# Second layer of three experts with weights stationary and tokens moving, and a second ring of raw expert weights

## The chip, the cores and the metric

The kernel runs on one core of one Trainium2 chip. The metric is device microseconds (us) of one execution, the median of several runs.

## The reference, cut to what matters

Attention with a threshold (4 x 8 heads, 576 places, 64 wide), then a dense layer of 2048 hidden units on the 2304 tokens of 512 numbers, then a layer of eight experts of which each token goes through one. The change touches the experts:

```python
e_idx = np.argmax(x @ w_gate, axis=1)
for e in range(8):
    mask = e_idx == e
    h = np.maximum(x[mask] @ w1[e], 0.0)      # 512 -> 1024
    ye = h @ w2[e]                            # 1024 -> 512
    out[mask] = gate_w[mask, None] * eom[mask, e, None] * ye
```

In the attention, scores below the row's maximum less tau are left out of the softmax:

```python
thresh = np.max(scores, axis=-1, keepdims=True) - tau
scores = np.where(scores >= thresh, scores, -1000000000.0)
```

## The kernel before, in words

**Stages.** Attention and a first part of the dense layer run mixed (to about 510 us), then the rest of the dense layer with the gates (to about 765 us), then the experts one after another. Nothing is emitted where it stands: the program collects operations with `sc.add(engine, duration, due, function, reads, writes)`, and a planner (`Sched`) sorts them. It simulates the engines with the durations given, so that each figure in an `sc.add` and in helpers such as `pool_tt`, `dve`, `act` and `mm` bears on the order of instructions on every engine. `dma` adds the issuing instruction (500 ns on SP, 1038 ns on POOL) and an entry "DQ" for the transfer, whose latency the planner knows. Buffers come in rings (`buf(pool, name, n, shape)`), and the n-th buffer behind one waits for all its users; the turn within a ring follows the order in which the program creates buffers. On the chip each engine works through its own instructions in the planner's order. Products are taken in three parts, of high and low halves: high x high, high x low, low x high.

**Experts.** Experts 1 to 7 are ordered by load and have room for 384, 384, 352, 320, 288, 288 and 256 tokens (`CAPS`, the first of its eight entries is expert 0's), thus expert 4 has tiles of 128, 128 and 64, experts 5 and 6 of 128, 128 and 32. `expert(e)` (L1459) does this:
- Tokens: a gather of rows per tile (L1473, POOL), turned by PE (L1480, 4 transposes into "pt", a ring of two PSUM banks), rounded into xh (ScalarE) and the rest into xl (VectorE).
- First layer (L1537): for each of 8 blocks of hidden units, 3 products x 4 pieces of 128 inputs; a 128x128 piece of w1 is stationary and the tokens (the cap) move, into "ph", a ring of two PSUM banks. ScalarE takes relu to hh (L1542), VectorE the rest to hl (L1544); so hidden units lie across the partitions.
- Second layer (L1565): for each block f and token tile j, three matmuls in which the tile's hh or hl is stationary (128 hidden units x tokens) and the 512 columns of w2 move, into bank "py" of tile j:

```python
for n, (x_, wx) in enumerate(((h_, w_h), (h_, w_l), (l_, w_h))):
    nc.tensor.matmul(py[j].t[0:size[j]], x_(), wx(), ...)
```

- Then ScalarE scales each tile by its tokens' gates to "o" (L1573), and POOL scatters the rows to the output (L1577).

**Weights.** `raw_of` (L1302) gathers 512 KB of raw weights, enough for two of the sixteen pieces of an expert, with an indirect transfer issued on POOL (L1316), into "wraw", a ring of two buffers. `weights` splits each piece into a high part (ScalarE L420 and VectorE L424 in turn) and a low part (VectorE L440), into a set of 23 buffers.

**Thresholds.** In `attention`, each tile of scores gets its maximum on VectorE (L959, with the em tile), the exponential on ScalarE (L962, e) and the threshold tb = maximum + tau on GpSimd (L970, one column); then VectorE masks and sums (L972) from em, tb and e. Which engine takes tb is the table entry `"thr": "P"`, whose letters are taken in turn (A: ScalarE, D: VectorE, P: GpSimd).

Of the kernel before, what the change touches and what calls it, by code (L numbers as in the profile page):

```python
# [16 lines left out]
AF = mybir.ActivationFunctionType  # L17
# [4 lines left out]
P = 128  # L22
# [28 lines left out]
NHH = 12  # L51
NRAW = 2
ENGINES = {
# [3 lines left out]
    "r_3": "PD", "p_x": "Z" * 50 + "X" * 10 + "Z" + "XX" + "Z" + "X" * 62 + "Z" + "X", "bot": "A", "sum": "D",  # L57
# [216 lines left out]
def pool_tt(n):  # L274
    return int(2.11 * n + (145 if n > 400 else 12))

# [41 lines left out]
def tile_main(ctx, tc, qa, qb, q0, kT, vv, tau, w_in, w_out, gates, w1, w2, out, dbg=None):  # L318
# [108 lines left out]
    def rest(cls, n, due, dst, src, hi, r, w, psum=False):  # L427
        eng = pick(cls) if cls in ENGINES else cls
        if eng == "POOL" and n > HALVE:
            def part(k):  # L430
                a, b, h_ = dst(), src(), hi().bitcast(F32)
                m = a.shape[1]
                cut = slice(0, (m + 1) // 2) if k == 0 else slice((m + 1) // 2, m)
                nc.gpsimd.tensor_tensor(out=a[:, cut], in0=b[:, cut], in1=h_[:, cut], op=ALU.subtract)

            for k in range(2):
                o = sc.add("POOL", pool_tt(n // 2) + 170, due, lambda k=k: part(k), r, w)
            return o
        e = nc.vector if eng == "DVE" else nc.gpsimd
        return sc.add(eng, dve(n, psum) + 5 if eng == "DVE" else pool_tt(n), due, lambda: e.tensor_tensor(  # L440
            out=dst(), in0=src(), in1=hi().bitcast(F32), op=ALU.subtract), r, w, port=not psum)

    def dma(due, fn, r, w, nbytes, eng="SP", slack=0, after=()):
        o = sc.add(eng, 1038 if eng == "POOL" else 500, due, fn, r, w, lat=480, after=after)
        if due < 0 and not after:
            opening.append(o)
        sc.add("DQ", nbytes // 250, due, lambda: None, r, w, lat=810 + slack)
        return o
# [141 lines left out]
    def step(c, p, first, last, hp, xp, due, span, low, half, wide=False):  # L590
# [17 lines left out]
        for j in range(2):  # L608
            for n, (w_, x_) in enumerate(((0, xh), (0, xl), (1, xh))):
                sc.add("PE", 460, due + k * q, lambda j=j, n=n, w_=w_, x_=x_: hmm(j, n, w_, x_), [wi, x_], [ph])  # L610
                k += 1
# [31 lines left out]
        for t in range(2):  # L643
            for n, (g_, w_) in enumerate(((gh, 0), (gh, 1), (gl, 0))):
                sc.add("PE", 464, d + k * q, lambda t=t, n=n, g_=g_, w_=w_: xmm(t, n, g_, w_),
                       [g_, wo], [x2b[c, half][t]])
                k += 1
# [257 lines left out]
    def attention(ui, k0, qs):  # L905
# [16 lines left out]
        for qt in range(2 + half):  # L922
# [4 lines left out]
            for h in range(1 if merged else 2):  # L927
# [37 lines left out]
                if eng == "ACT":  # L965
                    sc.add("ACT", 187, d + 801, lambda tb=tb, mx=mx: nc.scalar.activation(
                        tb.t, mx.t, AF.Identity, bias=tau_t), [mx], [tb])
                else:
                    e_ = nc.vector if eng == "DVE" else nc.gpsimd
                    sc.add(eng, 69 if eng == "DVE" else 150, d + 801, lambda tb=tb, mx=mx, e_=e_: e_.tensor_tensor(  # L970
                        out=tb.t, in0=mx.t, in1=tau_t, op=ALU.add), [mx], [tb])
# [8 lines left out]
            if eng == "ACT":  # L980
                sc.add("ACT", 200, dl + 1.3 * TAU, lambda rs=rs, m=m: nc.scalar.activation(
                    rs.t[:, 0:m], rs.t[:, 0:m], AF.Identity, bias=eps_t), (), [(rs, h) for h in range(m)])
            else:
                sc.add(eng, 71 if eng == "DVE" else 165, dl + 1.3 * TAU, lambda rs=rs, m=m, e_=e_: e_.tensor_scalar(
                    out=rs.t[:, 0:m], in0=rs.t[:, 0:m], scalar1=1e-9, scalar2=None, op0=ALU.add),
                    (), [(rs, h) for h in range(m)])
# [122 lines left out]
    k = 0  # L1109
# [187 lines left out]
    for k in range(NE):  # L1297
        begins.append(begins[k] + 96 * CAPS[k] / 2.4 + 24 * 693 * -(-CAPS[k] // P) / 3 + 1300)
    raws = {}
# [3 lines left out]
    def raw_of(i):  # L1303

        i //= 2
        if i not in raws:
            k, n = divmod(i, 8)
            raws[i] = raw = buf("wf", "wraw", 2, [P, 2 * DM])
            src, n = (w1, n) if n < 4 else (w2, n - 4)
# [149 lines left out]

    def expert(e):  # L1460
        due, cap = begins[e], CAPS[e]
        EX = begins[e + 1] - due
        half_ = 96 * cap / 2.4
        size = [min(P, cap - j * P) for j in range(-(-cap // P))]
        xh = buf("fx", "xh", 2, [P, 4, 384], F32R)
        xl = buf("fx", "xl", 2, [P, 4, 384], F32R)
        for j, m in enumerate(size):
# [19 lines left out]
            round_to("f_h", 4 * m, d, hi, src, [pt], [(xh, j)], True)  # L1487
            rest("p_l", 4 * m, d, lambda cols=cols: xl.t[:, :, cols], src, hi, [pt, (xh, j)], [(xl, j)], True)
        hid = {}
        for half in range(0 if e else 2):  # L1490
# [30 lines left out]
        for f in range(8):  # L1521
# [7 lines left out]
            ph = buf("ps_f", "ph", 2, [P, 512])  # L1529
            h_, l_ = (buf("fx", x, NHH, [P, 384], F32R) for x in ("hh", "hl"))  # L1530
            for j, m in enumerate(size):
                hid[f, j] = [(x, lambda x=x, j=j, m=m: x.t[:, j * P:j * P + m]) for x in (h_, l_)]
# [7 lines left out]
            for n, (wx, x_) in enumerate(((w_h, xh), (w_h, xl), (w_l, xh))):  # L1540
# [5 lines left out]
                [ph, h_], [l_])  # L1546
        py = [buf("ps_o", f"py{j}", 1, [P, DM]) for j in range(len(size))]
        for f in range(8):
            if 16 * e + 8 + f >= len(ws):
                ws.append(weights(16 * e + 8 + f))  # L1550
        tail = e == NE - 1
        turn_ = [(f, j) for f in range(8) for j in range(len(size))]
# [16 lines left out]
        for j, m in enumerate(size):  # L1569
            s_ = 3 * e + j  # L1570
            o_ = buf("fx", "o", 3, [P, DM])
            d = due + (half_ + (j + 1) * 5160 if tail else EX + j * 600)
            sc.add("ACT", act(512, True, True), d, lambda j=j, o_=o_, s_=s_, m=m: nc.scalar.activation(  # L1573
                o_.t[0:m], py[j].t[0:m], AF.Copy, scale=scl[0:m, s_:s_ + 1]), [py[j], (list_m, 2 if e else 5)], [o_])

            def scatter(o_=o_, s_=s_, m=m):
                r = nc.gpsimd.indirect_dma_start(  # L1577
                    out[:, :], bass.IndirectOffsetOnAxis(ap=ids[0:m, s_:s_ + 1], axis=0), o_.t[0:m], None,
                    bounds_check=NT - 1, oob_is_err=False)
                if s_:  # L1580
                    tc.declare_no_dep(r.ins, group="rows", reason="each token is in one place of one list")
                tc.add_to_no_dep_group("rows", r.ins)

            dma(d, scatter, [o_, (list_m, 0)], [sc.mem()], 262144, "POOL")

# [187 lines left out]
```

## Time and profile before

| | |
|---|---|
| median of three runs | 1036.72 us (1036.66 to 1038.6) |
| the profiled execution | 1037.6 us |
| its span, first to last instruction | 1035.7 us |
| mean granted clock of TensorE, share of full speed | 0.995 |
| busy: PE / loads of weights / VectorE / ScalarE / GpSimd | 97% / 86% / 76% / 58% / 49% |
| experts 1 to 7 with their end | from about 801 us on |

PE is TensorE's matmuls and PEld its loads of stationary data, DVE is VectorE, ACT ScalarE, POOL GpSimd. A line like L1565 is one of the kernel. "out<-in" are the tiles written and read, "x24" the number of instructions. "[2.71 <-DVE w L440]" says that the engine sat idle for 2.71 us ahead of this instruction, and what ended that. The ends of matmuls are modelled, so consecutive matmuls overlap in the rows: their pitch is read from the starts.

### The profile page before, as it was taken

The numbers are of one execution on the slowest core, as the hardware profiler recorded it, in microseconds if no ns is written. First come the engines' busy times: TensorE is split into PE (matmuls) and PEld (weight loads), VectorE is DVE, ScalarE is ACT, GpSimd is POOL, SyncE is SP. The second block draws the span as 40 slices with busy tenths as digits, with TensorE's granted clock in tenths as the row PEclk, the third lists the DMA queues.
The fourth block names the chain that finished last, engine by engine and source line by source line (L and its number), as shares of the span: only waits on it lengthen the run. The fifth ranks groups of instructions, "written<-read, shape, count | busy, mean of one in ns | idle before, by whom it ended". The sixth has DMA issues, their size and how long they took to land.

```text
span 1035.7 us, 18657 instructions
## 1 busy us (share of the span) xinstructions
PE 1000.7 (97%) x6535; PEld 887.9 (86%) x6535; DVE 785.3 (76%) x1938; ACT 601.6 (58%) x1218; POOL 504.4 (49%) x739
## 2 busy tenths in 40 slices
PE   6999999999999999999999999999999999899997
PEld 4778789999899999999989888888988898788786
DVE  5789989989999999988567976797465665566650
ACT  3779899989887877776454544444323333234321
POOL 2567989889879986555310100110105445344421
PEclk9999999999999999999999999999999999999999
DMA  8465454455646463352392742331506655465530
GB/s 213 137 199 185 130 177 144 151 160 157 215 145 219 147 220 123 107 196 93 135 378 89 278 139 83 129 106 65 221 32 202 183 169 179 123 189 183 171 121 30
DMA packets 45913, 163.69 MB, mean 158 GB/s; under 512 B 6462, under 2 KB 6462, under 8 KB 39920
## 3 DMA queue, kind: packets, MB, share of 16 engines
q1 hardware_dynamic: 34160, 122.60, 36.0%
q0 software_dynamic: 11488, 39.53, 12.2%
q8 instruction: 53, 0.87, 0.4%
q14 instruction: 52, 0.43, 0.1%
q10 hardware_dynamic: 160, 0.26, 0.1%
HBM read 127.24 MB, written 35.85 MB: 157 GB/s over the span
## 4 chain that ended last, share of the span: by engine, by line
PE 67%; DVE 12%; ACT 8%; issue 6%; POOL 3%; DMA 2%; another core or an unknown queue 1%; POOLq 0%; SPq 0%; ACTq 0%; DVEq 0%
PE x L636 16%; PE ph L602 15%; PE py L1565 10%; PE ph L1537 8%; PE pv L1056 5%; PE sp L941 4%; PE pt L1009 3%; DVE em L972 3%; DVE em L959 2%; PE sp L950 2%; ACT eth L420 2%; ACT e L962 2%; DVE etl L440 1%; PE ph L1242 1%; DMA wraw<-in_w_dram,widx 1%
## 5 line engine op out<-in xcount | busy, mean ns | idle before, releaser
L602 PE MATMUL ph<-xh,wi 128*128 128x256 f32 x1152 | 181.5, 286 | 0.0
L636 PE MATMUL x<-wo,gh 128*128 128x512 f32 x576 | 167.4, 403 | 0.0
L602 PEld LDWEIGHTS ph<-xh,wi 128*128 128x128 f32 x1152 | 157.3, 188 | 4.0
L972 DVE SCALAR_TENSOR_TENSOR em<-em,tb,e 128x576 f32<-128x576 f32 x144 | 138.6, 964 | 17.3 <-ACT e L962 12.4
L962 ACT ACTIVATE e<-em,mx 128x576 f32<-128x576 f32 x144 | 111.6, 775 | 44.7 <-DVE em L959 38.8
L422 POOL TENSOR_SCALAR gh<-u 128x512 fp32r<-128x512 f32 x52 | 39.9, 768 | 194.2 <-DVE u L625 147.4
L959 DVE TENSOR_SCALAR_CACHE_REDUCE em<-sp 128x576 f32<-128x576 f32 x144 | 107.7, 748 | 10.5 <-PE sp L950 8.9
L636 PEld LDWEIGHTS x<-wo,gh 128*128 128x128 f32 x576 | 100.2, 189 | 15.5
L1316 POOL DMA_INDIRECT wraw<-in_w_dram,widx x56 | 57.6, 1029 | 100.3 <-DVE w L440 46.8
L420 ACT ACTIVATE eth<-pt 128x512 fp32r<-128x512 f32 (+2 forms) x160 | 86.5, 550 | 13.8 <-PE pt L1009 7.2
L615 ACT ACTIVATE u<-ph 128x512 f32<-128x512 f32 x72 | 42.8, 596 | 87.8 <-PE ph L602 83.6
L602 PE MATMUL ph<-xl,wi 128*128 128x256 f32 x576 | 93.2, 283 | 0.0
L636 PE MATMUL x<-wo,gl 128*128 128x512 f32 x288 | 92.2, 404 | 0.0
L970 POOL TENSOR_TENSOR tb<-mx,tau_t 128x1 f32<-128x1 f32 x144 | 60.5, 420 | 61.7 <-DVE em L959 55.7
L1009 PE MATMUL pt<-ident,em 128*128 128x128 f32 x576 | 86.4, 277 | 3.6 <-ACT etl L420 1.9
L1009 PEld LDWEIGHTS pt<-ident,em 128*128 128x128 f32 x576 | 69.3, 143 | 13.6 <-DVE em L972 3.4
L602 PEld LDWEIGHTS ph<-xl,wi 128*128 128x128 f32 x576 | 79.4, 189 | 0.7
L1565 PE MATMUL py<-w,hh 128*128 128x512 f32 (+3 forms) x252 | 79.8, 398 | 0.0
L623 DVE SCALAR_TENSOR_TENSOR w<-w,u 128x512 f32<-128x512 f32 x72 | 51.0, 708 | 36.3 <-ACT w L619 36.2
L941 PE MATMUL sp<-kst,qh 128*128 128x288 f32 (+2 forms) x252 | 71.4, 302 | 1.8 <-DVE em L959 1.6
L941 PE MATMUL sp<-kst,ql 128*128 128x288 f32 (+2 forms) x252 | 68.0, 292 | 0.0
L440 DVE TENSOR_TENSOR w<-wraw,w 128x512 fp32r<-128x512 f32 x98 | 65.3, 696 | 2.1 <-ACT w L420 0.8
(376 smaller groups left out, 2428.9 us busy)
## 6 DMA issues: line engine op xcount, KB each, us to landing
wi<-wsv SPq DMA_DIRECT2D x17, 1024.0 KB, 5.4
wo<-wsv SPq DMA_DIRECT2D x17, 1024.0 KB, 5.3
craw<-in_w_in_dram SPq DMA_DIRECT2D x14, 512.0 KB, 4.5
craw<-in_w_out_dram SPq DMA_DIRECT2D x14, 512.0 KB, 4.4
kr<-in_kT_dram SPq DMA_DIRECT2D x24, 288.0 KB, 6.2
wsv<-wi SPq DMA_DIRECT2D x6, 1024.0 KB, 4.8
wsv<-wo SPq DMA_DIRECT2D x6, 1024.0 KB, 4.9
vr<-in_vv_dram SPq DMA_DIRECT2D x16, 320.0 KB, 3.1
```

Of the source, the lines that this page charges most:

```text
L420: return sc.add("ACT", act(n, psum), due, lambda: nc.scalar.activation(dst(), src(), AF.Copy), r, w)
L440: return sc.add(eng, dve(n, psum) + 5 if eng == "DVE" else pool_tt(n), due, lambda: e.tensor_tensor(out=dst(), in0=src(), in1=hi().bitcast ...
L602: nc.tensor.matmul(ph.t[:, j, :], wi.t[:, w_, cc * CH + j * P:cc * CH + (j + 1) * P], x_.t[:, cc, :], start=(n == 0 and cc == 0), stop=(n ...
L636: nc.tensor.matmul(x2b[c, half][t].t, g_.t[:, j, t * P:(t + 1) * P], wo.t[:, w_, j * DM:(j + 1) * DM], start=(first and n == 0 and j == 0) ...
L941: nc.tensor.matmul(sp.t[:, kb_, o:o + w], q_.t[:, q0:q0 + P], kb.t[:, hh, c0:c0 + w], start=(i == 0), stop=(i == len(todo) - 1),)
L959: sc.add("DVE", 665, d, lambda ev=ev, sp=sp, mx=mx: nc.vector.tensor_scalar(out=ev().rearrange("p (a b) -> p a b", a=2), in0=sp.t[:, :, 0: ...
L962: sc.add("ACT", 667, d + 800, lambda e=e, ev=ev, mx=mx: nc.scalar.activation(e.t, ev(), AF.Exp, bias=mx.t, scale=-1.0), [(em, h), mx], [e])
L970: sc.add(eng, 69 if eng == "DVE" else 150, d + 801, lambda tb=tb, mx=mx, e_=e_: e_.tensor_tensor(out=tb.t, in0=mx.t, in1=tau_t, op=ALU.add ...
L972: sc.add("DVE", 729, d + TAU, lambda ev=ev, tb=tb, e=e, rs=rs, h=h: nc.vector.scalar_tensor_tensor(out=ev(), in0=ev(), scalar=tb.t, in1=e. ...
L1009: nc.tensor.matmul(pt.t[:, kt, :], em.t[:, c0:c0 + P], ident, is_transpose=True, start=(kt == 0), stop=(kt == 3))
L1537: nc.tensor.matmul(ph.t[:, 0:cap], wx()[:, cc * P:(cc + 1) * P], x_.t[:, cc, 0:cap], start=(n == 0 and cc == 0), stop=(n == 2 and cc == 3))
L1565: nc.tensor.matmul(py[j].t[0:size[j]], x_(), wx(), start=(f == 0 and n == 0), stop=(f == 7 and n == 2))
```

## The change

The second layer of experts 4, 5 and 6 (`SWAP`) is done by a new function `swapped`: a 128x128 piece of w2 is stationary and the expert's tokens move, into four banks "py0" to "py3", one for each 128 outputs. ScalarE copies the banks to SBUF ("col", in buffers "u" and "w" of the dense layer), PE turns each token tile back into "pt" (4 transposes), and the scaled copy and the scatter, now a function `store`, read "pt". Two raw-weight buffers "wraw2" are added (`NSP`), which every second gather of experts 1 to 7 takes. The token step of the next expert (`tokens`) is created ahead of the second layer of this one, which sets its turn in the "pt" ring. In the figures of the planner: `begins` knows the shorter second layer; transfers issued on POOL land 1800 ns later (`FAR`); GpSimd's subtractions of up to 400 columns, matmuls of the dense layer and the small threshold and sum steps are given longer durations. Every third threshold is taken by ScalarE.

```diff
+SWAP = (4, 5, 6)
+FAR = 1800
+NSP = 2
...
-    "x_h": "AP", "x_l": "P", "w_h": "AD", "w_l": "D", "w_l0": "D", "f_h": "A", "thr": "P", "eps": "P", "r_2": "DA",
+    "x_h": "AP", "x_l": "P", "w_h": "AD", "w_l": "D", "w_l0": "D", "f_h": "A", "thr": "PPA", "eps": "P", "r_2": "DA",
...
 def pool_tt(n):
-    return int(2.11 * n + (145 if n > 400 else 12))
+    return int(2.11 * n + (145 if n > 400 else 110 if n < 256 else 60))
...
-                o = sc.add("POOL", pool_tt(n // 2) + 170, due, lambda k=k: part(k), r, w)
+                o = sc.add("POOL", pool_tt(n // 2) + 110, due, lambda k=k: part(k), r, w)
...
-        sc.add("DQ", nbytes // 250, due, lambda: None, r, w, lat=810 + slack)
+        sc.add("DQ", nbytes // 250, due, lambda: None, r, w, lat=810 + slack + (FAR if eng == "POOL" else 0))
...
-                sc.add("PE", 460, due + k * q, lambda j=j, n=n, w_=w_, x_=x_: hmm(j, n, w_, x_), [wi, x_], [ph])
+                sc.add("PE", 473, due + k * q, lambda j=j, n=n, w_=w_, x_=x_: hmm(j, n, w_, x_), [wi, x_], [ph])
...
-                sc.add("PE", 464, d + k * q, lambda t=t, n=n, g_=g_, w_=w_: xmm(t, n, g_, w_),
+                sc.add("PE", 468, d + k * q, lambda t=t, n=n, g_=g_, w_=w_: xmm(t, n, g_, w_),
...
-                    sc.add(eng, 69 if eng == "DVE" else 150, d + 801, lambda tb=tb, mx=mx, e_=e_: e_.tensor_tensor(
+                    sc.add(eng, 75 if eng == "DVE" else 300, d + 801, lambda tb=tb, mx=mx, e_=e_: e_.tensor_tensor(
...
-                sc.add(eng, 71 if eng == "DVE" else 165, dl + 1.3 * TAU, lambda rs=rs, m=m, e_=e_: e_.tensor_scalar(
+                sc.add(eng, 75 if eng == "DVE" else 220, dl + 1.3 * TAU, lambda rs=rs, m=m, e_=e_: e_.tensor_scalar(
...
-        begins.append(begins[k] + 96 * CAPS[k] / 2.4 + 24 * 693 * -(-CAPS[k] // P) / 3 + 1300)
+        l2_ = 96 * CAPS[k] / 2.2 + 1300 if k in SWAP else 24 * 693 * -(-CAPS[k] // P) / 3
+        begins.append(begins[k] + 96 * CAPS[k] / 2.4 + l2_ + 1300)
...
-            raws[i] = raw = buf("wf", "wraw", 2, [P, 2 * DM])
+            spare = NSP and k and i % 2
+            raws[i] = raw = buf("fx", "wraw2", NSP, [P, 2 * DM]) if spare else buf("wf", "wraw", 2, [P, 2 * DM])
...
+    def store(e, j, m, due, src, dep):
+        s_ = 3 * e + j
+        o_ = buf("fx", "o", 3, [P, DM])
+        sc.add("ACT", act(512, True, True), due, lambda: nc.scalar.activation(
+            o_.t[0:m], src(), AF.Copy, scale=scl[0:m, s_:s_ + 1]), [dep, (list_m, 2 if e else 5)], [o_])
...
+    def swapped(e, due, cap, size, py, hid):
+
+        step_ = 96 * cap / 2.2 / 8
+        for f in range(8):
+            w_, w_h, w_l = ws[16 * e + 8 + f]
+            h_, l_ = hid[f]
+            for n, (x_, wx) in enumerate(((h_, w_h), (h_, w_l), (l_, w_h))):
+                def lay2(f=f, n=n, x_=x_, wx=wx):
+                    for k in range(4):
+                        nc.tensor.matmul(py[k].t[:, 0:cap], wx()[:, k * P:(k + 1) * P], x_.t[:, 0:cap],
+                                         start=(f == 0 and n == 0), stop=(f == 7 and n == 2))
+
+                sc.add("PE", mm(cap, 4), due + (f + n / 3) * step_, lay2, [x_, w_], py)
+        d = due + 8 * step_
+        col = [buf("mo", "uw"[k // 2], 2, [P, DM]) for k in range(4)]
+        for k in range(4):
+            sc.add("ACT", act(cap, True), d, lambda k=k: nc.scalar.activation(
+                col[k].t[:, 0:cap], py[k].t[:, 0:cap], AF.Copy), [py[k]], [col[k]])
+        for j, m in enumerate(size):
+            pt = buf("ps_u", "pt", 2, [P, 4, P])
+
+            def turns(j=j, m=m, pt=pt):
+                for k in range(4):
+                    nc.tensor.transpose(pt.t[0:m, k, :], col[k].t[:, j * P:j * P + m], ident)
+
+            sc.add("PE", 434, d + 1500 + 500 * j, turns, col, [pt])
+            store(e, j, m, d + 2000 + 500 * j, lambda m=m, pt=pt: pt.t[0:m].rearrange("p a b -> p (a b)"), pt)
...
+        if e + 1 < NE:
+            tokens(e + 1)
-        py = [buf("ps_o", f"py{j}", 1, [P, DM]) for j in range(len(size))]
+        py = [buf("ps_o", f"py{j}", 1, [P, DM]) for j in range(4 if e in SWAP else len(size))]
...
+        if e in SWAP:
+            swapped(e, due + half_, cap, size, py, hid)
+            return
```

## Rows read from the trace of the kernel before

**Rows 1.** windows: stretch, us, busy of PE, PEld, DVE, ACT, POOL; clock, DMA, GB/s

```profile
100.00:200.00 100.00, 95.03 (x645) 85.22 (x644) 93.62 (x225) 92.80 (x189) 85.74 (x131) 1.00 0.49 156
...
200.00:300.00 100.00, 98.38 (x692) 90.73 (x691) 94.78 (x212) 86.97 (x177) 86.68 (x130) 1.00 0.56 177
...
850.00:900.00 50.00, 46.24 (x239) 41.05 (x238) 27.56 (x51) 16.10 (x30) 21.09 (x20) 0.97 0.49 151
...
790.00:1005.00 215.00, 209.72 (x1126) 180.18 (x1126) 130.32 (x238) 75.90 (x143) 92.74 (x89) 0.99 0.55 169
```

**Rows 2.** chain of waits, experts: start us, us, engine, tile, line, matmuls

```profile
822.06 15.40 PE py L1565 x66
...
914.43 3.52 PE ph L1537 x24
...
942.42 3.17 PE ph L1537 x24
```

**Rows 3.** timeline of PE, expert 4 to 5: start us, us, what

```profile
937.42 0.60 PE L1480 MATMUL pt<-ident,rows 128*128 128x128 f32 x4
...
937.77 0.70 PE L1565 MATMUL py<-w,hh 128*64 128x512 f32 x2
...
938.55 0.62 PE L1565 MATMUL py<-w,hh 128*128 128x512 f32 x2
```

**Rows 4.** groups by shape, ScalarE in the experts: busy us, mean ns

```profile
L1542 ACT ACTIVATE hh<-ph 128x288 fp32r<-128x288 f32 x16 | 6.4, 406 | 9.2 <-PE ph L1537 8.7 <-DVE w L424 0.4
...
L1573 ACT ACTIVATE o<-py,scl 128x512 f32<-128x512 f32 x19 | 13.0, 686 | 20.1 <-PE py L1565 17.9 <-issue 1.3 <-ACT xh L420 0.6
```

**Rows 5.** timeline, the end of the last expert's work

```profile
1028.26 0.39 PE L1565 MATMUL py<-w,hl 128*128 128x512 f32 x1
...
1028.73 0.69 ACT L1573 ACTIVATE o<-py,scl 128x512 f32<-128x512 f32 x1 [4.89 <-PE py L1565]
```

**Rows 6.** timeline of POOL, gathers of raw weights and rows

```profile
925.06 1.00 POOL L1316 DMA_INDIRECT wraw<-in_w_dram,widx  x1 [2.71 <-DVE w L440]
...
937.72 1.00 POOL L1316 DMA_INDIRECT wraw<-in_w_dram,widx  x1 [2.30 <-DVE xl L440]
...
939.02 1.01 POOL L1473 DMA_INDIRECT rows<-x2f,gid  x1 [0.30 <-issue]
```

**Rows 7.** waits from 790 to 1036 us: us in total, times, longest

```profile
ACT w L420 <- DMA wraw<-in_w_dram,widx: 59.6, 29, 5.4
...
POOL wraw L1316 <- DVE w L440: 45.4, 22, 3.2
```

**Rows 8.** chain of waits, the steps ahead of two stalls of PE

```profile
879.45 1.53 another core or an unknown queue
...
882.12 1.77 another core or an unknown queue
...
972.54 5.30 DMA wraw<-in_w_dram,widx
```

**Rows 9.** timeline, the matmuls behind these two stalls

```profile
884.99 0.91 PE L1537 MATMUL ph<-xh,w 128*128 128x352 f32 x4 [3.59 <-DVE hl L1544]
...
979.63 0.79 PE L1537 MATMUL ph<-xh,w 128*128 128x288 f32 x4 [0.47 <-DVE hl L1544]
```

**Rows 10.** tile tb: ns minimum, median, maximum; idle time of its instructions, times

```profile
L970 POOL TENSOR_TENSOR tb<-mx,tau_t x144: 179/270/1311, 9.3 to 495.0; 128x1 f32<-128x1 f32 x144
...
  ACT e L962: 12.4, 17
...
  POOL tb L970: 3.6, 6
```

**Rows 11.** groups by shape, small steps of ScalarE

```profile
L621 ACT ACTIVATION_READ_ACCUMULATOR gl<-u 128x1 f32 x72 | 13.6, 189 | 0.0
...
L994 ACT ACTIVATE rb<-rs 128x128 f32<-128x128 f32 x64 | 18.6, 303 | 4.2 <-PE pv L1087 2.6 <-DVE rs L987 1.3
```

**Rows 12.** groups by shape, loads of stationary weights in the first layer

```profile
L1537 PEld LDWEIGHTS ph<-xh,w 128*128 128x128 f32 x320 | 51.1, 191 | 7.3 <-DVE hl L1544 5.6 <-issue 0.3
```

More of the change, by code (lines that the diff above doesn't have):

```diff
@@ L1458, in tile_main, with scatter @@
     sc.gate = sc.barrier(to_f, 0, [o for o in sc.ops if o not in set()])
-    def expert(e):
+    def store(e, j, m, due, src, dep):
[3 more added lines that the diff above has]
+            o_.t[0:m], src(), AF.Copy, scale=scl[0:m, s_:s_ + 1]), [dep, (list_m, 2 if e else 5)], [o_])
+        def scatter():
+            r = nc.gpsimd.indirect_dma_start(
+                out[:, :], bass.IndirectOffsetOnAxis(ap=ids[0:m, s_:s_ + 1], axis=0), o_.t[0:m], None,
+                bounds_check=NT - 1, oob_is_err=False)
+            if s_:
+                tc.declare_no_dep(r.ins, group="rows", reason="each token is in one place of one list")
+            tc.add_to_no_dep_group("rows", r.ins)
+        dma(due, scatter, [o_, (list_m, 0)], [sc.mem()], 262144, "POOL")
@@ L1461, in expert, with tokens @@
+    xs_ = {}
+    def tokens(e):
         due, cap = begins[e], CAPS[e]
-        EX = begins[e + 1] - due
-        half_ = 96 * cap / 2.4
         size = [min(P, cap - j * P) for j in range(-(-cap // P))]
@@ L1488, in expert @@
             rest("p_l", 4 * m, d, lambda cols=cols: xl.t[:, :, cols], src, hi, [pt, (xh, j)], [(xl, j)], True)
+        xs_[e] = xh, xl
+    def expert(e):
+        due, cap = begins[e], CAPS[e]
+        EX = begins[e + 1] - due
+        half_ = 96 * cap / 2.4
+        size = [min(P, cap - j * P) for j in range(-(-cap // P))]
+        if not e:
+            tokens(e)
+        xh, xl = xs_[e]
         hid = {}
@@ L1530, in expert @@
             h_, l_ = (buf("fx", x, NHH, [P, 384], F32R) for x in ("hh", "hl"))
+            hid[f] = h_, l_
             for j, m in enumerate(size):
@@ L1569, in expert @@
         for j, m in enumerate(size):
-            s_ = 3 * e + j
-            o_ = buf("fx", "o", 3, [P, DM])
             d = due + (half_ + (j + 1) * 5160 if tail else EX + j * 600)
[L1573 to L1584, printed above, removed]
+            store(e, j, m, d, lambda j=j, m=m: py[j].t[0:m], py[j])
     for e in range(NE):
```

## The prediction

> **What bounds the kernel now.** I read the windows view first. The reader is to see two things in it: TensorE is busy for practically the whole of every stretch behind the first 100 us, and what is missing is small and sits in two places. In the attention stage (100 to 300 us) it lacks 5.0 and 1.6 us per hundred, while VectorE, ScalarE and GpSimd are at 85 to 95% there; in the expert stage (790 to 1005 us), which the edit rebuilds, it lacks 5.3 us of 215, 3.8 of them between 850 and 900 us [rows 1]. Busy PE is not PE at its peak, so I next took the pitch of dense matmuls from the chain of waits: 66 matmuls with 512 moving columns took 15.40 us, 233 ns each; 24 with 320 columns took 3.52 us, 147 ns each; 24 with 288 columns took 3.17 us, 132 ns each [rows 2]. So PE's time follows the columns that move (0.45 ns each, nearly nothing besides), and an expert is bound by its sum of moving columns. That makes any column removed in this stage worth its full price, as long as ScalarE, VectorE and the gathers keep ahead.
>
> **The second layer of experts 4, 5 and 6.** Before, each token tile is stationary and the weights' 512 columns move: 8 blocks of hidden units x 3 tiles x 3 products = 72 matmuls x 233 ns = 16.8 us per expert, and a tile of 64 or 32 tokens costs as much as one of 128. After, a 128x128 piece of the weights is stationary and the 320 or 288 token places move: 8 x 3 x 4 = 96 matmuls. They have the shapes of the first layer of the same expert, so its pitch prices them: expert 4 96 x 147 ns = 14.1 us (2.7 us less), experts 5 and 6 96 x 132 ns = 12.7 us (4.1 us less each) [rows 2]. Sum: 10.9 us less. Its lower bound is zero, if the pitch were kept by something else; I know no row that says so.
>
> **Turning back.** The result lies with the outputs across the partitions, so ScalarE copies four banks to SBUF and PE turns them back, 4 transposes for each of 3 tiles and 3 experts, 9 groups. The nearest row is the group that turns the gathered tokens: from its start to the start of the second group of three behind it 1.13 us pass, and a group of three takes 3 x 233 ns = 0.70 us, so that the transposes cost 0.43 us [rows 3]. A short tile can only be cheaper. 9 x 0.43 = 3.9 us more on PE. Net on PE: 10.9 - 3.9 = 7.0 us less.
>
> ScalarE gets 4 copies per expert, each like the hh copy of 128x288, 406 ns: 1.6 us. The scaled copies to "o" (686 ns each) stay as many, but read the turned bank [rows 4]. ScalarE is busy 76 of 215 us here [rows 1], so its total is no matter; its order is. The copies stand in one in-order queue with the hh copies of the next expert's first layer, and PE has only two "ph" banks, so it can run two blocks (3.17 us at 288 columns [rows 2]) before an hh copy is due. I cost this at nothing: 1.6 us lie under 3.17 us, and the second layer's work of the next expert can be pulled forward. If that cover is gone, PE waits for four copies and a hand-over at each of the three seams: 1.6 us, and some 0.5 us for the hand-overs between engines (an estimate: ScalarE's copy starts 0.47 us behind the start of the last matmul, which itself still drains [rows 5]), 2.1 us x 3 = 6.3 us. A fourth bank "py3" is taken and each expert's successor writes "py0" only half an expert later, so the banks are no wait.
>
> **Two rings of raw weights and the moved token step.** Half of the gathers of experts 1 to 7 get buffers of their own, four in all. Now the queue of gathers runs in lockstep with the splitting: five gathers in a row were issued from 925.06 to 937.72 us, 3.17 us apart, most after a wait for VectorE's last split of an earlier buffer [rows 6, 7]. Eight of them make 25.3 us; behind the change an expert of 288 places needs 12.7 + 12.7 us of matmuls and two times 1.3 us of transposes, 28.0 us. Two buffers would thus only just have fed it, with six gathers and scatters of rows at about 1.3 us in the same POOL queue not counted; four buffers take this away, and POOL's own work, 14 x 1.3 us = 18 us, is then the limit of the supply. The added transfers in flight I cost at nothing: the DMA share of this stage is 0.55 [rows 1].
>
> What can be won besides is the idle PE time of the stage. Of it 0.47 us, before the matmul at 979.63, ends a chain that runs through the landing of a raw buffer (5.3 us) [rows 8, 9]. The largest stall, 3.6 us before the matmul at 884.99, ends a chain of ScalarE steps with 1.5 and 1.8 us for "an unknown queue" between them [rows 8, 9]; the profile shows ScalarE waiting for raw weights 59.6 us in 29 waits as the head of its queue, with hh copies behind it [rows 7]. Planned landing of gathers is put 1.8 us later, so these splits will stand later in ScalarE's queue. The ends are nothing won, or all 5.3 us [rows 1], or 2 us lost if a new order makes another such stall; I take the one that is the ring's own, 0.5 us.
>
> **The figures of the plan and the thresholds.** The order of the whole program is planned from these figures, so every stage is ordered anew. One of three "tb" (144 in all) goes from GpSimd to ScalarE. GpSimd's last from 179 to 1311 ns; VectorE's masking step waits for them 6 times, 3.6 us in all, and 17 times, 12.4 us, for the exponential on ScalarE [rows 10]. A third of the former is 1.2 us won. On ScalarE the step comes in line with the exponential; no row shows it with one column, but reading an accumulator of one column takes 189 ns and a 128x128 copy 303 ns [rows 11]. The nearer row is 189 ns: 48 x 17/144 = 6 waits made longer by 0.19 us, 1.1 us lost. I take zero; the ends are 6.6 us won (all idle PE of 100 to 300 us) and, with each of 48 steps at 0.25 us in series on the path, 12 us lost. The longer figures for matmuls (473 for 460) only order things.
>
> The end is left alone: the last expert is not turned, and its last matmul, copy and scatter follow each other without anything to wait for [rows 5].
>
> **The sum.** The profiled execution took 1037.6 us, its span 1035.7 us, 1.9 us lying around it; it is 0.9 us above the median 1036.7 us. 1037.6 - 7.0 - 0.5 = 1030.1 us for such an execution, and 0.9 us less for the median: 1029.2, say 1029 us.
>
> **Rivals.** (1) The stalls go too: the stage loses its 5.3 us of idle time as well, or the attention stage a like amount. For it: the waits of ScalarE for raw weights, and that planning with later landings puts the waits elsewhere. Against: "unknown queue" is not a raw buffer. 1036.7 - 7.0 - 5.3 = 1024 us. (2) The seams: PE waits there for four copies. For it: one in-order ScalarE queue and two "ph" banks. Against: 3.17 us of cover. 1036.7 - 7.0 + 6.3 = 1036 us. (3) Slower: the 48 thresholds in series with the exponential. In 100 to 200 us ScalarE is at 93% and VectorE at 94% [rows 1]; if each masking step that loses its parallel GpSimd step starts 0.25 us later and VectorE has nothing to put there, 12 us are lost, and beyond 7.0 us of it (28 of the 48) the change loses altogether: 1036.7 - 7.0 + 12 = 1042 us. Against: only 17 of 144 such steps wait for ScalarE's exponential now. (4) Weight loads are not hidden: 24 more per expert at 191 ns each [rows 12], 72 x 0.191 = 13.8 us more, 1036.7 - 7.0 + 13.8 = 1043 us. Against it: a pitch of 132 ns is shorter than one load of 191 ns, so loads and matmuls of this very shape overlap [rows 2, 12]. The Trainium skill ("TensorE: Matmul & The Clock Gate", Part 3: Packing small matmuls — row/col tiling) says that weight loads overlap with matmuls in flight only when their row groups differ, which would speak against more loads; these rows differ from it, and the measurement decides. (5) The gain isn't on the path: supply or splitting takes over and the experts keep their length, 1036 us. Against: 18 us of POOL for 28 us.
>
> **How the numbers follow.** Forecast (1026 to 1033 us) 0.53, (1) 0.15, (2) 0.13, (3) 0.08, (4) 0.03, (5) 0.08. About 0.2%, or 2 us, is what a measurement of this kernel can tell from no change. Faster by more (below 1034.6 us): the forecast, (1), and half of (2) and (5), where part is kept: 0.78. Slower by more (above 1038.8): (3) and (4), 0.11. The same: the remaining 0.11. The range reaches down over (1) and up to (2): 1021 to 1036 us.
>
> **What would show it.** The new matmuls of experts 4 to 6 at 147 and 132 ns in runs of 24; nine groups of 128-column transposes at 0.43 us; no idle PE of over 1 us between the last of them and the next expert's first layer; gathers bunched in fours with shorter waits of ScalarE for them; PE idle of 100 to 300 us within 3 us of now. The forecast is wrong if the pitch of the new matmuls is nearer to 233 ns, if the seams show waits for ScalarE, or if the attention stage ends more than 3 us earlier or later than now.

## The result, and the profile after

The changed kernel takes **1026.09 us** in the median (1025.14 to 1028.62, 6 runs) beside 1036.96 us for the kernel before (1034.88 to 1038.86, 6 runs): ratio 0.9892, interval 0.9871 to 0.9913. That is 10.9 us less; forecast were 7.7 us less, 1029 us, range 1021 to 1036. The profiled execution of after took 1026.68 us with a span of 1024.8 us (before: 1037.6 and 1035.7).

The chip matters for what follows. The runs above and the three sets of experiments ran on chips on which the kernel before takes 1037.0, 1036.6, 1028.6 and 1038.1 us, so a kernel is compared with the runs of before in its own set, and kernels with each other inside a set.

Line numbers of after stand a little lower in the code than those of before: masking L975 (was L972), thresholds L969 on ScalarE and L973 on GpSimd (L970), first layer L1598 (L1537), hh and hl L1603 and L1605 (L1542, L1544), old second layer L1631 (L1565), gather of raw weights L1321 (L1316). New are L1490 (second layer with weights stationary), L1497 (its banks to SBUF) and L1504 (turning back).

**Where the time went**, by three marks in the two profiled executions: the end of the last masking step on VectorE, the first weight load of the experts' first layer, and the span's end.

| | before | after | difference |
|---|---|---|---|
| last masking step ends | 497.2 | 489.9 | -7.3 |
| from there to the experts' first weight load | 304.0 | 304.7 | +0.7 |
| experts, to the span's end | 234.5 | 230.2 | -4.3 |
| span | 1035.7 | 1024.8 | -10.9 |

So most of the gain came in the attention stage, which the forecast put at nothing, and the experts gave 4.3 us of 7.5. The windows view of after (stretch, us, busy of PE, PEld, DVE, ACT, POOL; clock, DMA, GB/s) shows both; its lines answer to [rows 1]:

```profile
100.00:200.00 100.00, 97.57 (x651) 86.57 (x652) 93.48 (x221) 95.14 (x203) 81.76 (x121) 1.00 0.48 152
200.00:300.00 100.00, 99.13 (x708) 91.95 (x707) 94.59 (x221) 88.72 (x187) 85.95 (x124) 1.00 0.54 177
850.00:900.00 50.00, 50.00 (x258) 44.10 (x257) 30.62 (x54) 15.55 (x29) 17.67 (x17) 1.00 0.51 161
790.00:1005.00 215.00, 207.38 (x1294) 193.29 (x1293) 128.09 (x236) 80.32 (x159) 91.35 (x87) 0.99 0.52 163
```

TensorE lacks 2.4 and 0.9 us in 100 to 300 us where it lacked 5.0 and 1.6. In the experts it lacks **more** than before, 7.6 us for 5.3, though the 3.8 us between 850 and 900 us are gone: they were not cured, they went elsewhere. The new work itself is in the chain of waits of after (start us, us, engine, tile, line, matmuls), beside [rows 2] and [rows 3]:

```profile
842.22 2.48 issue
844.70 3.76 PE ph L1598 x12
...
922.37 9.97 PE py L1490 x68
...
938.82 0.44 PE pt L1504 x4
...
940.31 0.87 PE pt L1504 x8
...
953.02 9.60 PE py L1490 x72
```

68 matmuls of 320 columns in 9.97 us are 147 ns each, 72 of 288 columns in 9.60 us are 133 ns, and a group of four transposes takes 0.44 us: each of these three prices is the forecast's. The first two lines are what spoiled the stage: 2.5 us of nothing, and then 12 matmuls of 384 columns in 3.76 us, 313 ns each, where 24 of them take 4.20 us elsewhere in that chain, 175 ns.

A weight load of the new matmuls, in the groups by shape (busy us, mean ns | idle before), answers to [rows 12]:

```profile
L1490 PEld LDWEIGHTS py<-hh,w 128*128 128x128 f32 x136 | 19.8, 188 | 0.0
```

188 ns each under a pitch of 133 to 147 ns, with no idle before any of them: loads overlap here with matmuls of the same row group. The rule of the Trainium skill ("TensorE: Matmul & The Clock Gate", Part 3: Packing small matmuls — row/col tiling), that they do so only where the row groups differ, does not hold for these instructions; by it the kernel would have been slower, rival (4). The same section of the Trainium skill also lets a load into a background weight buffer be pulled ahead of matmuls in flight, which would fit; no run here shows that this is what happens.

### The profile page after: what moved, and what is told of

The parts are those of the page before. It is cut to its first block, busy times and chain, and to the rows that moved or that the text cites. A ratio compares the mean times of both kernels' runs of the same rounds, so it can differ in the third digit from the quotient of the medians.

```text
span 1024.8 us, 18910 instructions
## 1 busy us (share of the span) xinstructions
PE 991.6 (97%) x6643; PEld 896.2 (87%) x6643; DVE 777.7 (76%) x1938; ACT 611.4 (60%) x1278; POOL 494.0 (48%) x691
## 4 chain that ended last, share of the span: by engine, by line
PE 80%; ACT 7%; DVE 6%; issue 4%; DMA 1%; POOL 1%; SPq 0%; another core or an unknown queue 0%; POOLq 0%; ACTq 0%; DVEq 0%
PE x L639 18%; PE ph L605 18%; PE ph L1598 9%; PE pv L1059 7%; PE py L1631 7%; PE sp L944 5%; PE pt L1012 4%; PE py L1490 4%; ACT e L965 2%; PE sp L953 2%; DVE em L975 1%; ACT eth L423 1%; DVE em L962 1%; PE ph L1245 1%; ACT etl L423 1%
## 5 line engine op out<-in xcount | busy, mean ns | idle before, releaser
L639 PE MATMUL x<-wo,gh 128*128 128x512 f32 x576 | 169.7, 405 | 0.0
L975 DVE SCALAR_TENSOR_TENSOR em<-em,tb,e 128x576 f32<-128x576 f32 x144 | 134.1, 935 | 15.8 <-ACT e L965 8.2
L965 ACT ACTIVATE e<-em,mx 128x576 f32<-128x576 f32 x144 | 111.4, 774 | 37.3 <-DVE em L962 29.4
L962 DVE TENSOR_SCALAR_CACHE_REDUCE em<-sp 128x576 f32<-128x576 f32 x144 | 107.9, 749 | 13.5 <-PE sp L953 10.5
L1321 POOL DMA_INDIRECT wraw<-in_w_dram,widx x56 | 60.7, 1083 | 78.5 <-DVE hl L1605 23.6
L1603 ACT ACTIVATE hh<-ph 128x384 fp32r<-128x384 f32 (+4 forms) x56 | 24.6, 442 | 71.9 <-PE ph L1598 62.3
L1598 PE MATMUL ph<-xh,w 128*128 128x288 f32 (+4 forms) x320 | 59.1, 316 | 3.4 <-issue 3.1
```

What stands on the lines that cost most here:

```text
L639: nc.tensor.matmul(x2b[c, half][t].t, g_.t[:, j, t * P:(t + 1) * P], wo.t[:, w_, j * DM:(j + 1) * DM], start=(first and n == 0 and j == 0) ...
L962: sc.add("DVE", 665, d, lambda ev=ev, sp=sp, mx=mx: nc.vector.tensor_scalar(out=ev().rearrange("p (a b) -> p a b", a=2), in0=sp.t[:, :, 0: ...
L965: sc.add("ACT", 667, d + 800, lambda e=e, ev=ev, mx=mx: nc.scalar.activation(e.t, ev(), AF.Exp, bias=mx.t, scale=-1.0), [(em, h), mx], [e])
L975: sc.add("DVE", 729, d + TAU, lambda ev=ev, tb=tb, e=e, rs=rs, h=h: nc.vector.scalar_tensor_tensor(out=ev(), in0=ev(), scalar=tb.t, in1=e. ...
L1598: nc.tensor.matmul(ph.t[:, 0:cap], wx()[:, cc * P:(cc + 1) * P], x_.t[:, cc, 0:cap], start=(n == 0 and cc == 0), stop=(n == 2 and cc == 3))
```

## The experiments

### One part alone, on the chip with 1036.6 us

Two kernels halve the change: the experts' part with the old figures and thresholds, and the figures and thresholds with the old experts.

```diff
 experts_only (from after)
-"thr": "PPA"
+"thr": "P"
 ... all planned durations as in the kernel before
 front_only (from after)
-SWAP = (4, 5, 6)
-FAR = 1800
-NSP = 2
+SWAP = ()
+FAR = 0
+NSP = 0
```

> The expert edits and both rings with the later landing of gathers, but all thresholds on GpSimd and the old figures of the plan elsewhere. By my sum, which put nothing on the attention, this gives the whole 7.5 us: 1029 us, the first expert's matmuls starting at about 801 us as before. By the trace of after, where the experts start 6.5 us earlier and gain only 4.4 us themselves: about 1032.5 us. If the orders hang together by chance alone, the attention's end moves by some us either way.

Measured 1024.07 us (1022.3 to 1030.0), ratio 0.9895 (0.9856 to 0.9935).

> The other half: every third threshold on ScalarE and all new figures, but the old second layer, one ring, no later landing. If the 6.5 us lie in the attention: last masking step at about 490 us, 1030.5 us. By my sum: nothing, 1036.7 us.

Measured 1027.18 us (1024.7 to 1028.6), ratio 0.9910 (0.9879 to 0.9941). Its masking ends at 489.0 us, experts_only's at 495.5. Each half alone gives about what the whole gives: 12.6 and 9.5 us here, 10.9 for both in the first comparison. So the front part is real and is worth a gain of its own, which the forecast had denied, and something in the experts moves by several us between executions, which hides the sum: TensorE lacks 2.1 us in 790 to 1005 us of the profile of experts_only, and 7.6 us in that of after. The two that follow split the front part.

```diff
 thr_back (from after)
-"thr": "PPA"
+"thr": "P"
 thr_only (from before)
-"thr": "P"
+"thr": "PPA"
```

> The whole change, but all thresholds back on GpSimd, with the new figures. Theory A (the gain in the attention is the thresholds moved off GpSimd): last masking step back at about 497 us, 1033 us. Theory B (it is the truer figures of the plan): stays at about 490 us, 1026 us. Theory C (chance of the order): something else, by more than 2 us from both.

Measured 1028.54 us (1025.3 to 1031.0), ratio 0.9923 (0.9897 to 0.9949).

> The kernel before with every third threshold on ScalarE and nothing else, the figures old. Theory A: last masking step at about 490 us, 1030 us. Theory B: about 497 us, 1037 us. My rival of thresholds in series: later than 497 us, above 1039 us.

Measured 1037.14 us (1035.4 to 1040.6), ratio 1.0012 (0.9991 to 1.0033). Neither the new figures nor the new thresholds bring the gain by themselves. After's own threshold steps, in the view of tile tb (duration ns minimum/median/maximum, first and last start; then VectorE's idle time ahead of masking by its releaser, us and times), answer to [rows 10]:

```profile
L975 DVE DVE_READ_ACCUMULATOR em<-em,tb,e x144: 70/77/85, 10.9 to 489.9; 128x1 f32 x144
L973 POOL TENSOR_TENSOR tb<-mx,tau_t x96: 181/193/1093, 9.3 to 485.7; 128x1 f32<-128x1 f32 x96
L969 ACT ACTIVATE tb<-mx,tau_t x48: 278/284/312, 16.3 to 488.8; 128x1 f32<-128x1 f32 x48
its engine sat idle before it (us, times) until:
...
  ACT e L965: 8.2, 11
  ACT tb L969: 3.8, 5
...
  POOL tb L973: 1.1, 3
```

A threshold on ScalarE lasts 284 ns, not 189; VectorE waits 5 times for it, and for the exponential and both kinds of threshold together 13.1 us instead of 16.0 [rows 10]. That is a small gain, as estimated, and it is not what moved the stage. In thr_only the same waits sum to 14.8 us, and yet its last masking step ends where before's does. The ends of masking in the four kernels, from the same view (thr_only, thr_back, front_only; the last line is thr_300, below):

```profile
L972 DVE DVE_READ_ACCUMULATOR em<-em,tb,e x144: 71/77/89, 11.2 to 497.3; 128x1 f32 x144
...
L975 DVE DVE_READ_ACCUMULATOR em<-em,tb,e x144: 70/77/86, 11.0 to 495.1; 128x1 f32 x144
...
L975 DVE DVE_READ_ACCUMULATOR em<-em,tb,e x144: 70/77/86, 11.3 to 489.0; 128x1 f32 x144
...
L972 DVE DVE_READ_ACCUMULATOR em<-em,tb,e x144: 71/77/87, 11.5 to 496.0; 128x1 f32 x144
```

### One part back, on the chip with 1028.6 us

On this chip executions differ by less, and after gains more.

> The changed kernel unchanged, profiled once more. If the stalls in its experts (2.5 us at 844.7, three of about 1 us) belong to its order of instructions, they stand at the same places with the same lengths and the experts take 230 us again; if they belong to the execution, they move, and the experts take anything between 223 us (as with the thresholds and figures of before) and 234 us.

Measured 1015.11 us (1014.7 to 1015.4), ratio 0.9865 (0.9851 to 0.9879), 13.5 us less than before.

```diff
 no_swap (from after)
-SWAP = (4, 5, 6)
+SWAP = ()
 one_ring (from after)
-NSP = 2
+NSP = 0
 far0 (from after)
-FAR = 1800
+FAR = 0
```

> The whole change without the turned second layer. By my sum of matmuls and transposes this costs 7.0 us: 1033 us, the new matmuls and the nine turning groups gone, experts 4 to 6 at 16.8 us each for their second layer. If the gain of the expert stage came from the rings, about 1027 us.

Measured 1021.35 us (1020.9 to 1022.7), ratio 0.9928 (0.9914 to 0.9941). The rebuilt second layer is worth 1021.35 - 1015.11 = 6.2 us, against 7.0 forecast. In both profiles TensorE is busy through the whole stage, so this is the difference of work, not of stalls.

> The whole change with one ring of two raw buffers. My sum put 0.5 us on the rings: about 1026.6 us, ScalarE waiting for raw weights some 60 us in all again, with hardly a wait of PE behind it. The rival that a shorter expert is bound by its supply: experts 5 and 6 at up to 33 us instead of 28, 1031 us or more.

Measured 1028.74 us (1026.4 to 1030.2), ratio 0.9996 (0.9986 to 1.0006). Without the second ring the whole change is worth **nothing**: 13.6 us lost against after_again, of which 10.8 us in the experts (230.8 for 220.0 us) and 2.8 us ahead of them. Of the 10.8 us, 5.1 are lost in experts 5 and 6 and 5.0 in the last expert, whose own work the change leaves alone. The windows of after_again, no_swap and one_ring, in this order:

```profile
790.00:1005.00 215.00, 214.63 (x1343) 200.79 (x1342) 128.75 (x236) 81.57 (x161) 92.48 (x88) 1.00 0.51 165
...
790.00:1005.00 215.00, 215.00 (x1208) 187.62 (x1207) 128.43 (x236) 77.36 (x149) 91.49 (x87) 1.00 0.51 164
...
790.00:1005.00 215.00, 210.80 (x1317) 195.65 (x1315) 123.20 (x233) 81.13 (x163) 90.81 (x88) 1.00 0.51 161
```

What holds one_ring is seen in its waits from 790 to 1036 us (us in total, times, longest):

```profile
POOL wraw L1321 <- DVE w L443: 51.5, 22, 4.8
...
ACT w L423 <- DMA wraw<-in_w_dram,widx: 42.3, 17, 5.0
```

and in its timeline of POOL, and of PE at the start of the last expert's second layer:

```profile
941.62 1.00 POOL L1321 DMA_INDIRECT wraw<-in_w_dram,widx  x1 [1.11 <-DVE xl L443]
...
947.64 1.00 POOL L1321 DMA_INDIRECT wraw<-in_w_dram,widx  x1 [5.01 <-DVE xl L443]
...
961.58 1.00 POOL L1321 DMA_INDIRECT wraw<-in_w_dram,widx  x1 [4.12 <-DVE w L443]
...
974.03 1.01 POOL L1321 DMA_INDIRECT wraw<-in_w_dram,widx  x1 [2.57 <-ACT hh L1603]
```

```profile
1005.53 0.49 PE L1631 MATMUL py<-w,hh 128*128 128x512 f32 x1 [1.67 <-ACT w L423]
1006.86 0.50 PE L1631 MATMUL py<-w,hh 128*128 128x512 f32 x1 [0.84 <-DVE w L443]
```

A gather waits for VectorE's last split of the buffer it refills, the splits wait for the gather, and in the end PE waits for the splits: the lockstep of [rows 6, 7], now on the path. From the gather at 941.62 to the eighth behind it at 974.03 us 32.4 us pass, with three scatters of rows between them, and expert 5 takes 32.0 us in this kernel (28.6 in after_again), expert 6 28.8 us (27.2). In after the same waits of ScalarE for raw weights sum to almost nothing, where [rows 7] had 59.6 us in 29:

```profile
ACT w L423 <- DMA wraw<-in_w_dram,widx: 2.4, 2, 1.4
```

One_ring keeps the later planned landing (FAR); both taken away together wasn't tried, so how much of the 13.6 us comes from a plan that counts on later landings is not shown.

> The whole change with the landing of gathers planned as early as before. If the later landing only moves ScalarE's splits out of the way of its other work: ScalarE waits for raw weights by some tens of us again, PE's idle time in the experts grows by 1 to 3 us, 1027 to 1029 us. If four buffers do that by themselves: 1026 us and no such waits.

Measured 1015.99 us (1015.8 to 1016.5), ratio 0.9875 (0.9860 to 0.9889): the later planned landing is worth about 0.9 us (the runs of the two kernels don't overlap, the intervals of their ratios do). ScalarE's waits for raw weights in "w" are 7.6 us in 6 without it, so it is the buffers and not the plan that took them away.

### What moves between executions, on the chip with 1038.1 us

Three questions were left: which of the figures goes with the thresholds; whether columns price a fourth expert too; and what the late starts in the experts are. Of the last, after shows this (timeline of all engines):

```profile
843.57 0.49 ACT L1603 ACTIVATE hh<-ph 128x384 fp32r<-128x384 f32 x1 [4.59 <-PE ph L1598]
...
844.15 1.01 POOL L1321 DMA_INDIRECT wraw<-in_w_dram,widx  x1 [0.30 <-ACT hh L1603]
...
844.70 1.20 PE L1598 MATMUL ph<-xh,w 128*128 128x384 f32 x4 [2.48 <-issue]
...
847.91 0.49 ACT L1603 ACTIVATE hh<-ph 128x384 fp32r<-128x384 f32 x1 [3.33 <-remote]
```

PE stops at 842.22 us (the chain above), so the block of 12 matmuls ahead of its last one ended near 840.1 (2.1 us per block); ScalarE, idle since 838.97, copies it only at 843.57, some 3 us late. PE has two such banks and stands still for 2.5 us, until VectorE too has read the bank. The next copy, of the block that was done at 842.22, starts at 847.91 with ScalarE idle for 3.3 us ahead of it. Behind the idle time PE's matmuls are slow, and the granted clock in the windows around it says why: between its two levels of 1.2 and 2.4 GHz it is mixed there, and full otherwise.

```profile
835.00:844.50 9.50, 7.22 (x45) 6.87 (x44) 6.11 (x13) 3.48 (x7) 7.37 (x8) 1.00 0.77 235
844.50:849.00 4.50, 3.76 (x12) 3.26 (x12) 1.92 (x5) 0.56 (x2) 2.93 (x3) 0.62 0.89 269
849.00:855.00 6.00, 5.96 (x34) 5.96 (x35) 3.91 (x8) 2.51 (x5) 1.23 (x1) 1.00 0.40 111
```

GpSimd issues one indirect transfer after the other through these stretches (8 in the first), and the DMA share is at 0.8 to 0.9. The "unknown queue" steps of 1.5 and 1.8 us ahead of before's large stall [rows 8, 9] look the same. They are no matter of order alone: thr_back and after have the same order of PE's instructions in the experts, and idle 5.5 and 7.6 us in 790 to 1005 us; after and after_again are one kernel, 7.6 and 0.4 us on two chips. So the raw weights were taken off GpSimd: in hw_gather they come by plain transfers from SP's queue, in the fixed order of the experts and not in that of their sizes, so that most experts work with another's weights, by the same instructions and bytes.

```diff
 thr_300 (from before)
-"thr": "P"
+"thr": "PPA"
-69 if eng == "DVE" else 150        # planned length of a threshold
+75 if eng == "DVE" else 300
 swap_3456 (from after)
-SWAP = (4, 5, 6)
+SWAP = (3, 4, 5, 6)
 hw_gather (from after)
-dma(due, gather, [widx], [raw], 524288, "POOL")
+dma(due, lambda ...: nc.sync.dma_start(raw.t, src[k, n]), [widx], [raw], 524288)
```

> The kernel before with two edits of the attention: every third threshold on ScalarE, and the figure for those left on GpSimd 300 ns instead of 150 (75 for 69 if VectorE took it). Neither thresholds alone (last masking step at 497.3 us, as before) nor the figures alone (495.1) brought the gain, both together did (488.5 to 490). If these two figures are the pair: last masking step at about 490 us, 6 to 8 us less than before. If the figures for matmuls or for GpSimd's other work are needed: about 497 us and no gain.

Measured 1036.66 us (1030.5 to 1042.6), ratio 0.9989 (0.9969 to 1.0010). The thresholds with their own planned lengths are not enough either.

> The whole change with expert 3 (352 places) turned as well. By the pitch (0.45 ns for each moving column) 96 matmuls of 160 ns are 15.4 us against 16.8, the turning takes 1.3 us of it back: 0.1 us less, thus the time of the changed kernel within its scatter. If a turned seam costs more than its transposes (ScalarE's copies): 0.5 us or more slower.

Measured 1024.55 us (1022.1 to 1025.8), ratio 0.9872 (0.9849 to 0.9895). Expert 3, with 352 columns, takes 32.3 us where after's takes 32.7. After itself wasn't in this set; its ratio of 0.9892 elsewhere has an interval that overlaps, so a fourth expert can't be told from three, as the sum says: 96 matmuls of 352 columns against 72 of 512, and 1.3 us of turning, cancel.

> The whole change, but the raw weights of experts 1 to 7 come over SP's queue in the fixed order of the experts (so the k-th largest expert gets the weights of expert k: this part of the computation is changed), and GpSimd issues the gathers and scatters of rows alone. If GpSimd's gathers make the late starts of ScalarE in the experts, those of over 1.5 us behind an unknown releaser are gone and the stage takes at most 221 us wherever the changed kernel shows them; if not, they stay. Where the changed kernel shows none: the same time.

Measured 1018.6 us (1017.7 to 1020.8), ratio 0.9824 (0.9802 to 0.9846), 6.0 us less than swap_3456 on the same chip. The windows of swap_3456 and hw_gather:

```profile
790.00:1005.00 215.00, 209.31 (x1342) 199.16 (x1341) 128.82 (x236) 82.16 (x164) 90.68 (x88) 0.98 0.52 164
...
790.00:1005.00 215.00, 214.63 (x1342) 200.50 (x1340) 126.43 (x232) 79.86 (x159) 38.55 (x37) 1.00 0.51 163
```

That is 5.3 us less idle time, and a full clock. (Swap_3456 has 0.1 us of its own in work, by the sum above.) ScalarE still stands idle four times for 1.2 to 1.5 us in hw_gather's experts, and none of it reaches PE. At the place of after's stall, swap_3456 has (timeline)

```profile
841.15 0.49 ACT L1603 ACTIVATE hh<-ph 128x384 fp32r<-128x384 f32 x1 [3.88 <-issue]
...
842.29 0.97 PE L1598 MATMUL ph<-xh,w 128*128 128x384 f32 x4 [1.75 <-issue]
```

and hw_gather

```profile
841.72 0.49 ACT L1603 ACTIVATE hh<-ph 128x384 fp32r<-128x384 f32 x1 [1.59 <-PE ph L1598]
842.16 0.85 PE L1598 MATMUL ph<-xh,w 128*128 128x384 f32 x4
```

> The kernel before, unchanged, one more profile on the same chip as the three others. Where ScalarE starts late in the experts there, PE idles for 5 us and the stage takes 234 us as in the profile of before; on a chip like that of the second set of runs about 228 us, with the last masking step at 496 us.

Measured 1034.18 us in one run, span 1032.4 us; in its experts TensorE lacks 4.9 us, with ScalarE idle for 4.0 us ahead of one copy, which starts 3.5 us behind the block that it copies. The stage takes 232 us and not 234: the granted clock is 1.00 from 790 to 1005 us here, so no matmuls are slowed. So this chip does show the late starts, and they went when GpSimd's gathers did. What in these gathers does it, the indirect form, GpSimd's queue or the bunching, was not separated. Hw_gather is also planned anew, with the transfers on another queue and without the later landing, and its PE works in another order than that of swap_3456 or after; only after and after_again, one order with 7.6 and 0.4 us, speak against the order as the cause. The gathers are not enough by themselves, nor is a high DMA share: at the same place of the program after_again, with the same gathers, and hw_gather, with an even busier DMA, have no stall (windows of the two, in this order):

```profile
835.50:840.00 4.50, 4.50 (x28) 4.50 (x27) 3.81 (x8) 1.50 (x3) 3.56 (x4) 1.00 0.82 243
...
835.50:840.00 4.50, 4.50 (x27) 4.36 (x26) 1.95 (x5) 1.37 (x3) 0.00 (x0) 1.00 0.93 315
```

## Why the prediction was right, point by point

The time fell into the range on the side of the forecast, but its sum, -7.5 us and -0.9 for the median, was made of terms of which one was right, one far too small for what it stood for, and one wrongly zero. The measured 1026.1 us lies at the edge of the forecast's own 1026 to 1033, 2 us from rival (1); that the sum comes so near is luck. In the profiled execution the experts gave 4.3 us of 7.5, the attention stage 6.6 to the experts' start instead of 0.

- **The new matmuls: right.** 147 and 133 ns were forecast from first-layer matmuls of the same shape, and measured. Turning cost 0.44 us per group for 0.43. The difference of the two, 7.0 us, measured 6.2 on the chip where TensorE doesn't stall. Of the missing 0.8 us one seam explains 0.4 (next point); the rest I can't place.
- **The seams cost nothing: right for the copies.** Of the three, one shows a wait, and it is hardly one for the copies. In after's timeline at the seam of experts 5 and 6, and in the last line in that of after_again:

```profile
965.55 0.43 PE L1530 MATMUL pt<-ident,rows 32*128 32x32 f32 x4
966.02 0.28 ACT L423 ACTIVATE xh<-pt 128x128 fp32r<-128x128 f32 x1
966.35 0.80 PE L1598 MATMUL ph<-xh,w 128*128 128x288 f32 x4 [0.37 <-ACT u L1497]
...
954.71 0.80 PE L1598 MATMUL ph<-xh,w 128*128 128x288 f32 x4 [0.37 <-ACT xh L423]
```

The label of the first names ScalarE's copy, but what came last is xh of the expert's last token tile, as the label in after_again says: PE turns that tile from 965.55 for 0.43 us, ScalarE rounds it at 966.02, right behind two of the four copies, and the matmul starts at 966.35. The wait is 0.37 us, in place of the 2.1 us per seam of rival (2). First-layer matmuls of the next expert stand between the last L1490 and the first L1504, as the forecast supposed.

- **The rings, 0.5 us: the mis-sized term.** The mechanism was named (two buffers in lockstep with the splits, 25.3 us for eight gathers where the shortened expert needs 28.0), and the step that failed is "would only just have fed it". I priced the ring by what idle time it could take from the kernel before, but its worth is what the change loses without it: 13.6 us (with FAR kept). The 25.3 us were a mean without the six gathers and scatters of rows in the same queue, which I mentioned and did not count; put behind one another with six at 1.3 us they make 33 us, longer than the 28.0 us of the expert. The kernel before shows it too: from the gather at 913.46 us to the eighth behind it at 942.90 us 29.4 us pass, with two scatters and three gathers of rows between them (timeline of POOL):

```profile
913.46 1.02 POOL L1316 DMA_INDIRECT wraw<-in_w_dram,widx  x1 [0.31 <-issue]
...
942.90 1.52 POOL L1316 DMA_INDIRECT wraw<-in_w_dram,widx  x1 [0.30 <-issue]
```

One_ring showed 32.4 us, with three such steps in place of six, so the sum of 33 us fits it in size and not in its parts. That sum stood in the prediction's own numbers: rival (5) is true of the kernel with one ring and false of the kernel with two.
- **The attention stage, 0: wrong.** It ended 7.3 us earlier, and "more than 3 us earlier or later" was among the signs of error. The estimate for the threshold alone, -1.2 and +1.1 us, is what thr_only shows, no change (ratio 1.0012), though 189 ns was too little for the step itself (284 ns). What I left out is the plan: a new order of the whole program, which I let count for nothing with an end of 6.6 us. The eight profiles with both the thresholds and all the new figures end masking at 487.5 to 491.4 us, the six without one or both at 495.1 to 497.3. In 100 to 500 us TensorE's busy time is, for before, thr_only and after:

```profile
100.00:500.00 400.00, 392.19 (x2755) 361.52 (x2754) 372.63 (x862) 328.81 (x672) 314.45 (x497) 1.00 0.49 158
...
100.00:500.00 400.00, 391.90 (x2740) 358.65 (x2739) 368.24 (x856) 331.06 (x706) 298.41 (x455) 1.00 0.47 156
...
100.00:500.00 400.00, 396.57 (x2794) 366.74 (x2795) 368.69 (x866) 336.66 (x716) 302.98 (x460) 1.00 0.48 157
```

4.4 us of idle time are gone from before to after, and 4.7 from thr_only to after, whose thresholds are the same. Which of the other figures (those for matmuls, for GpSimd's subtractions, for the small step "rs") does it, or whether one order just happens to fit, **stays open**.

- **The stalls of the experts: 5.3 us were bounded rightly, but taken for a matter of buffers or order.** Neither makes them by itself: with four buffers ScalarE's waits for raw weights vanished (59.6 to 2.4 us) and the stalls grew to 7.6 us, and one order idles 7.6 and 0.4 us on two chips. Slow matmuls come on top, but in both profiles: before has 24 in 5.67 us for 3.84 behind the stall of [rows 9], 1.8 us, after 12 in 3.76 us for 2.10, 1.7 us. The forecast left that price out, and it cancels in the difference. The clock of before there, in its windows:

```profile
884.90:891.00 6.10, 6.01 (x27) 5.92 (x28) 3.12 (x7) 1.29 (x3) 1.03 (x1) 0.72 0.28 86
```

What counts is the 2.3 us of idle time more (the ring's 0.5 us is part of that account): -7.0 + 2.3 = -4.7, or -3.9 with the 6.2 us of no_swap, and -4.3 was measured. On the chip where after_again shows hardly any of them the change is worth 13.5 us.
- **The end: right.** From the last copy on ScalarE to the end of the span before takes 7.0 us [rows 5], after 6.7 (it starts at 1018.08 us).
- **The rivals.** (2), (3) and (4) are dead: a seam of 0.37 us, VectorE waiting for thresholds and exponential 2.9 us less instead of 12 more, loads hidden. (1) is half true: the attention stage gained "a like amount", as its second clause has it, and the stalls stayed; (5) holds without the second ring.

So the total came out near by two errors of opposite sign, 6.6 us won that weren't forecast and 3.2 us of the experts' gain not kept.

## What to carry to other kernels

Price a part that feeds another by the time without it, not by the idle time that it could remove from the kernel as it is: count the whole queue that supplies a stage, every row gather and scatter in it, against the stage's new length. Matmul time follows the columns that move, and the nearest row of the same shape prices a rebuilt loop to within a few ns per matmul. Where an edit touches the numbers that a whole program is ordered by, a zero for the other stages is a guess: leave several us either way, and look at every stage's end before crediting the part that you meant to change.

## What the runs showed of the hardware that was not expected

- ScalarE can stand idle for up to 4.7 us (thr_back, ahead of its copy at 848.90 us) where no operand that the profile knows is missing ("issue" and "remote"), in the stretches looked at while GpSimd issues indirect transfers back to back. TensorE's idle time in 790 to 1005 us, much of it behind such starts, was 2.1 to 7.6 us over the profiles with these gathers on the other chips, and 0.4 us on the chip of 1028.6 us, for the very kernel that has 7.6 elsewhere; with the weights fetched over SP's queue it was 0.4 us on a chip that shows it (1018.6 us for 1024.55). A kernel with this order of experts read by a register and plain transfers would be the next thing to build; it was not tried.
- Behind such a stall the granted clock was 0.62 for 4.5 us, and matmuls of 384 columns took 313 ns instead of 175; in before, 0.72 for 6.1 us.
- The same kernel differs by nearly 1% between chips (1028.6 and 1038.1 us) in the median, and its executions spread by 0.3% on the one and 0.6% on the other. It is not the chip alone: on the chip of 1036.6 us one of 22 executions took 1028.5 us at a mean granted clock of 0.999, and one 1042.3 us at 0.992.
- A ScalarE step on one column lasts 284 ns; a 128x288 copy 410 to 423 ns.
